# An adaLN transformer block on one core: the opening of the forward attention in written order on all engines, with the first two head pairs run together

## The chip, the cores and the metric

The kernel runs on one core of a Trainium2 chip. The time is that of one execution on the device, in microseconds; less is better. The profile is of one execution, taken by the hardware profiler, and its span runs from the first to the last instruction of that execution.

## What is computed

The reference is one block of a conditioned transformer, forward and backward (ten outputs: the block's result and nine gradients). B=1, S=2048, D=512, H=32 heads of 16, F=1792, all in bf16. Cut to the part that matters here:

```python
sa, ca, ga, sb, cb, gb = split(silu(c) @ w_mod)
h   = layernorm(x) * (1 + ca) + sa
q, k, v = split(h @ wqkv)                 # 32 heads of 16
o   = softmax(q @ k.T * 16**-0.5) @ v
x   = x + ga * (o @ wo)
x   = x + gb * mlp(layernorm(x) * (1 + cb) + sb)
# outputs: x and the gradients of A_x, wqkv, wo, w1, b1, w2, b2, c, w_mod
```

## The kernel before

The forward attention (`phase_fwd`, L265) works on four query chunks of 512 rows (`qc`), in each on eight groups of four heads (`g`), in each on two head pairs (`jp`). One such step is called `n` here: n=0 is chunk 0, group 0, first pair; n=1 the second pair; n=2 the first pair of group 1; n=16 opens the second query chunk. A step has 16 units, one per block of 128 keys (`kb`). A unit is two matmuls for the scores of two heads (L349, PSUM tile `st`), one exponential of 128x1024 on ACT (L352, to `pu`), and eight small matmuls of probabilities by values (PV, L314), two to four units later. At a step's end DVE divides by the row sums (L321, L322).

Into the units a `Background` of generators puts other matmuls: `step(1.2)` lets 1.2 matmuls' worth of credit into each unit of the first query chunk. For that chunk the generator is `gen_qkv` (L545). For each group g from 1 to 7 it makes the queries of chunk 0, the keys of all 2048 rows, then some small work, then queries of the group before for the other chunks. One projection of 512 rows is `gen_fm` (L519): four matmuls (L526), an eviction by DVE (L535), a store of the feature-major result to DRAM by SP (L536, `QTq_d` or `KTq_d`), and a token-major form: a DMA transpose on SP (L538, `ev_tm`, three buffers), a copy on POOL (L540) and a store from POOL's queue (L542). Each matmul is one `yield 1`. The small work is: the modulation for the later stages after group 2 (`gen_mod`); for groups 3 to 6 the transposed values of 512 rows (`gen_vt`, L575: four times two POOL copies into one of two `vpad` tiles, L583 and L584, and a DMA transpose on SP, L585, to `vT`; then one store on POOL's queue, L587); a scaled copy of weights on POOL for groups 3 to 6 (L565, `wm_s`), transposed on SP (L560) and stored by POOL's queue (L562, `WmT_d`) one group later. `gen_vt` lets a unit pass after each of its four blocks.

The queries of a step stand in two of four tiles `QTm`, zero outside one head's 32 rows. They are loaded for the step after by `load_q` (L295), two small DMAs on POOL's queue, which the program calls at unit 8 of each step. Only a step's first pair of a later chunk loads its keys from DRAM as well (`load_k`, L301); within the first chunk the keys are already in a tile.

The opening (`gen_open`, L389) comes before all this and runs into n=0. It loads x, the weights and part of `w_mod`, forms silu(c) and the first modulation columns (`silu_c`, `mod_cols`), runs two times ten matmuls that only warm PE, normalizes the first 512 rows (`norm`), transposes and scales them (`turn`, to `xm1T`), and projects keys and queries of group 0. Then come, chopped into n=0's units by the counts in `opening` (L330), for each further 512 rows: norm, transposes, a value matmul row by row (`values`, L472, four matmuls and an eviction into `Vaug`, by turns on ACT and DVE), and the key projection. `mps`, the PSUM pool of all these, has two buffers.

What sets the order: a `manual_schedule` for PE and SP around the forward and phase 5 (L160) keeps these two engines' instructions in the order of the program. DVE, ACT and POOL are ordered by the tile framework's scheduler, which may put an instruction, DMAs on POOL's queue among them, ahead of others written before it.

Of the kernel before, what the change touches and what calls it, by code (L numbers as in the profile page):

```python
# [10 lines left out]
F32 = mybir.dt.float32  # L11
# [10 lines left out]
EPS = 1e-5  # L22

# [81 lines left out]
class K:  # L105
# [159 lines left out]
    def phase_fwd(self):  # L265
# [21 lines left out]
        QTm = []  # L287
        for j in range(4):
            t = fw.tile([P, 512], BF16, name=f"QTm{j}")
            nc.vector.memset(t[:], 0.0)  # L290
            QTm.append(t)
# [36 lines left out]
        first = self.gen_open(Vaug, KT, QTm, stp)  # L328
        next(first)
        opening = [9 + DT + DT * 4] * (SC - 1) + [4 * DT + 1]  # L330
        for n, (qc, g, jp) in enumerate(order):
            if (qc, g, jp) == (1, 0, 0):
                bg.drain()
                self.close_qkv()
                self.open_mlp()
                bg.add(self.gen_weights())
            accb = accp.tile([P, 512], F32, name="accbank")
            acc = accb[:, 0:8 * (DH + 1)].rearrange("p (a s e) -> p a s e", a=2, s=4)
            self.cur_g = g
            for kb in range(ST):  # L340
                if kb == ST // 2 and n + 1 < len(order):
                    if n < 2 * NQ - 1 and jp == 1:
                        bg.until(g + 1)
                    load_q(*order[n + 1])
                    if jp == 1:
                        KTn = load_k(*order[n + 1][:2])
                stt = stp.tile([P, 2, 512], F32, name="st")
                for a in range(2):
                    nc.tensor.matmul(stt[:, a, :], lhsT=KT[:, kb * P:(kb + 1) * P], rhs=QTm[2 * jp + a][:],  # L349
                                     start=True, stop=True)  # L350
                pu = pup.tile([P, 2, 512], BF16, name="pu")
                nc.scalar.activation(pu[:], stt[:], ACT.Exp, scale=self.scale)  # L352
                u = (n, qc, g, jp, kb, acc, pu)
                now = n * ST + kb
                pend.extend((u, a, sub) for a in range(2) for sub in range(4))
                if n == 0:
                    left = opening[kb // 4]
                    take = -(-left // (4 - kb % 4))
                    opening[kb // 4] -= take
                    for _ in range(take):  # L360
                        next(first)
                rate = (1.14 if qc else 1.2) if n or kb > 11 else 0
                room = int((SPAN - 2 - bg.plan(rate)) / PVT)
                while pend:
                    age = now - (pend[0][0][0] * ST + pend[0][0][4])
                    if age < 2 or (room <= 0 and age < 4):
                        break
                    pv(pend.pop(0))
                    room -= 1
                if rate:  # L370
                    bg.step(rate)
            if jp == 1 and n + 1 < len(order):
                if n < 2 * NQ - 1:
                    bg.until(-(g + 1))
                KT = KTn
# [13 lines left out]
    def gen_open(self, Vaug, KT, QTm, stp):  # L389
# [28 lines left out]
        nc.sync.dma_start(self.wmod[:, :, 2 * D:6 * D], wmod_v[:, :, 2 * D:6 * D])  # L418
        self.silu_c(ps)
        warm = ps.tile([P, 512], F32, name="pps")  # L420
        for _ in range(10):
            nc.tensor.matmul(warm[:], lhsT=self.ones_b[:], rhs=QTm[0][:], start=True, stop=True)
        for t in (1, 0):
            nc.vector.memset(self.wpad0[t][:], 0.0)
        nc.vector.memset(Vaug[:, :, :, DH:DH + 1], 1.0)
        nc.scalar.memzero(wpads[1][:])
        self.mod_cols(ps, (0, 1))
        warm = ps.tile([P, 512], F32, name="pps")
        for _ in range(10):
            nc.tensor.matmul(warm[:], lhsT=self.ones_b[:], rhs=QTm[0][:], start=True, stop=True)  # L430
# [6 lines left out]
        def norm(s4):  # L437
            b = slice(s4, s4 + 4)
            for st in range(s4, s4 + 4):
                nc.vector.bn_stats(stats[:, st, :], x0[:, st, :])  # L440
                nc.vector.bn_aggr(mv[:, st, :], stats[:, st, :])
            nc.vector.tensor_scalar(ve[:, b], mv[:, b, 1], EPS, None, ALU.add)
            nc.gpsimd.tensor_tensor(self.rstd1[:, b], ve[:, b], self.mhalf[:], ALU.pow)
            if s4 == 0:
                nc.vector.scalar_tensor_tensor(nmr[:, b], mv[:, b, 0], -1.0, self.rstd1[:, b], ALU.mult, ALU.mult)
            for st in range(s4, s4 + 4):
                if s4 == 0 and st % 2 == 0:
                    nc.scalar.activation(xhat1[:, st, :], x0[:, st, :], ACT.Identity, bias=nmr[:, st:st + 1],
                                         scale=self.rstd1[:, st:st + 1])
                else:  # L450
                    nc.vector.tensor_scalar(xhat1[:, st, :], x0[:, st, :], mv[:, st, 0:1], self.rstd1[:, st:st + 1],
                                            ALU.subtract, ALU.mult)
            nc.sync.dma_start(self.xhat1_d.rearrange("(st p) d -> p st d", p=P)[:, b, :], xhat1[:, b, :])

        def turn(s4, k2):
            tp = ps.tile([P, 2, 512], BF16, name="pps")
            for kt in range(2):
                for k in range(4):
                    nc.tensor.transpose(tp[:, kt, k * P:(k + 1) * P],
                                        xhat1[:, s4 + k, (k2 + kt) * P:(k2 + kt + 1) * P], self.ident[:])  # L460
                yield 0
                yield 0
            for kt in range(k2, k2 + 2):
                dst = xm1T[:, kt, s4 * P:s4 * P + 512]
                if kt % 2:
                    nc.vector.tensor_scalar(dst, tp[:, kt - k2, :], self.opcaT[:, kt:kt + 1], self.mod_col(0)[:, kt:kt + 1],
                                            ALU.mult, ALU.add)
                else:
                    nc.scalar.activation(dst, tp[:, kt - k2, :], ACT.Identity, bias=self.mod_col(0)[:, kt:kt + 1],
                                         scale=self.opcaT[:, kt:kt + 1])  # L470

        def values(s4, s5):  # L472
            for st in range(s4, s5):
                pt = ps.tile([P, 512], F32, name="pps")
                for kt in range(DT):
                    nc.tensor.matmul(pt[:], lhsT=xm1T[:, kt, st * P:(st + 1) * P], rhs=wq[:, kt, 2 * D:3 * D],
                                     start=(kt == 0), stop=(kt == DT - 1))
                    if kt == DT - 1:
                        (nc.scalar.copy if st % 2 else nc.vector.tensor_copy)(Vaug[:, st, :, 0:DH], pt[:].rearrange("p (h d) -> p h d", d=DH))
                    yield 0  # L480

        norm(0)
        for t in (1, 0):
            nc.gpsimd.tensor_copy(self.wpad0[t][:].rearrange("p k (j e) -> p k j e", e=32)[:, :, :, 0:DH],
                                  wq[:, :, t * D:t * D + 4 * DH].rearrange("p k (j d) -> p k j d", d=DH))
        for k2 in range(0, DT, 2):
            for _ in turn(0, k2):
                pass
        for _ in self.gen_fm(ps, 1, 0, 0, dst=KT[:, 0:512]):
            pass  # L490
        for _ in self.gen_fm(ps, 0, 0, 0, masked=QTm):
            pass
        nc.scalar.memzero(wpads[0][:])
        for t in (1, 0):
# [4 lines left out]
        for t in self.vpads:  # L499
            nc.gpsimd.memset(t[:], 0.0)  # L500
            nc.gpsimd.memset(t[:, :, :, DH:DH + 2], 1.0)
        yield 0
        for s4 in range(4, ST, 4):
            norm(s4)
            for k in range(2):
                yield from turn(s4, 2 * k)
                yield from values(s4 - 4 + k, s4 - 3 + k)
            yield from self.gen_fm(ps, 1, 0, s4 * P, dst=KT[:, s4 * P:s4 * P + 512])
            yield 0
            yield from values(s4 - 2, s4)  # L510
        yield from values(ST - 4, ST)
# [7 lines left out]
    def gen_fm(self, ps, t, g, s0, dst=None, masked=None):  # L519
# [5 lines left out]
        for kt in range(DT):  # L525
            nc.tensor.matmul(pt[:], lhsT=self.wpads[t][:, kt, g, :] if g else self.wpad0[t][:, kt, :], rhs=self.xm1T[:, kt, s0:s0 + 512],  # L526
                             start=(kt == 0), stop=(kt == DT - 1))
            yield 1
        if masked:
            for j in range(2):  # L530
                nc.scalar.copy(masked[j][32 * j:32 * j + 32, :], pt[32 * j:32 * j + 32, :])
        if dst is None:
            ev = eb.tile([P, 512], BF16, name="ev_fm")
            dst = ev[:]
        nc.vector.tensor_copy(dst, pt[:])  # L535
        nc.sync.dma_start((self.QTq_d, self.KTq_d)[t][g, :, s0:s0 + 512], dst)  # L536
        tm = eb.tile([P, 4, 4, 32], BF16, name="ev_tm")
        nc.sync.dma_start_transpose(tm[:].rearrange("p s j e -> p s (j e)"), dst)  # L538
        tmc = eb.tile([P, 4, 4, DH], BF16, name="ev_tmc")
        nc.gpsimd.tensor_copy(tmc[:], tm[:, :, :, 0:DH])  # L540
        w = 4 * DH
        nc.gpsimd.dma_start((self.qtm_d, self.ktm_d)[t][g, :, s0 // P * w:(s0 // P + 4) * w],  # L542
                            tmc[:].rearrange("p s j d -> p (s j d)"))
# [1101 lines left out]
```

The softmax here doesn't subtract the row's maximum and nothing guards it: scores larger than these inputs give would overflow.

## Time and profile before

| | us |
|---|---|
| runs | 2647.73, 2642.17, 2647.95 (median 2647.73) |
| profiled execution: time, span | 2644.01, 2642.2 |
| PE busy | 2485.0 (94%) |
| ACT busy | 2297.5 (87%) |
| DVE busy | 1767.7 (67%) |
| POOL busy | 408.4 (15%) |

By stretches of the span (busy time of each engine; the PE clock is the granted one):

| stretch | PE | DVE | ACT | POOL | clock | DMA share |
|---|---|---|---|---|---|---|
| 0 to 33 us | 22.20 | 25.27 | 14.19 | 18.68 | 0.90 | 0.76 |
| 33 to 66 | 28.41 | 11.77 | 22.21 | 5.75 | 1.00 | 0.28 |
| 66 to 132 | 64.20 | 17.26 | 65.41 | 22.01 | 1.00 | 0.42 |
| 132 to 198 | 61.74 | 14.57 | 65.78 | 30.26 | 1.00 | 0.82 |
| 198 to 264 | 62.73 | 15.65 | 65.41 | 30.40 | 1.00 | 0.84 |

The first query chunk of the attention lasts until some 284 us, the forward's attention until 997 us. In a line of the timeline the columns are start, duration, engine, line of the program, operation, output and inputs, and in brackets the idle time of the engine before it and what ended it. Matmuls are pipelined, so durations of neighbours overlap; the distance of their starts is what one costs. A PE that is shown as busy need not be at its limit.

### The profile page before, as it was taken

The page shows a single profiled execution, that of the slowest core. Times are in us where ns is not written, and L with a number is a line of the kernel's source. Part 1 is how long each engine was busy: PE and PEld are TensorE (multiplying, and loading weights), DVE is VectorE, ACT ScalarE, POOL GpSimd, SP SyncE. Part 2 cuts the span into 40 slices and gives each one's busy share as a digit, 9 for nine tenths or more (in the row PEclk, how much of TensorE's full clock was granted, in tenths as well). Part 3 has the DMA queues.
Part 4 walks back from the last instruction along what each step waited for, and adds up shares of the span by engine and source line. Part 5 has one row for each costly group of instructions (what it writes and reads, how often), then busy time and mean ns, then how long its engine had stood idle before and what let it go on. Part 6 is the DMA issues. An engine that isn't in the chain of part 4 may idle for free. (4 is left out here: it accounts for less than half of the span.)

```text
span 2642.2 us, 76655 instructions
## 1 busy us (share of the span) xinstructions
PE 2485.0 (94%) x31000; PEld 1230.0 (47%) x31231; DVE 1767.7 (67%) x3653; ACT 2297.5 (87%) x3712; POOL 408.4 (15%) x678
## 2 busy tenths in 40 slices
PE   7999999999999999899999999999999999999997
PEld 3555555555555554663444344434444434443443
DVE  5222223423323344658999999999999999999867
ACT  5999999999999995318999999999999999999823
POOL 3344521310221121350000000000000000000031
PEclk9999999999999999999999999999999999999999
DMA  5488752440441245999999999999999999999986
GB/s 166 100 162 191 176 105 78 116 102 23 127 117 52 79 105 132 222 235 186 202 199 201 199 201 197 198 197 207 200 200 198 202 200 202 197 201 206 206 224 166
DMA packets 1197811, 441.16 MB, mean 167 GB/s; under 512 B 1134958, under 2 KB 1159024, under 8 KB 1197456
## 3 DMA queue, kind: packets, MB, share of 16 engines
q1 hardware_dynamic: 1167584, 347.42, 71.9%
q0 software_dynamic: 29872, 88.83, 11.5%
q8 instruction: 244, 4.00, 0.6%
q14 instruction: 111, 0.91, 0.1%
HBM read 83.30 MB, written 68.69 MB: 58 GB/s over the span
## 5 line engine op out<-in xcount | busy, mean ns | idle before, releaser
L1310 DVE TENSOR_TENSOR ds<-dp,pu 128x512 bf16<-128x512 f32 x2048 | 1243.7, 682 | 55.1 <-PE dp L1308 47.5
L1367 ACT ACTIVATE pu<-st 128x512 bf16<-128x512 f32 x2048 | 1082.4, 613 | 122.1 <-PE dp L1308 63.1
L352 ACT ACTIVATE pu<-st 128x1024 bf16<-128x1024 f32 x1024 | 944.6, 1072 | 18.4 <-PE st L349 15.8
L349 PE MATMUL st<-QTm,KTq 128*128 128x512 bf16 x1920 | 580.7, 378 | 30.0 <-ACT pu L352 7.2
L314 PEld LDWEIGHTS <-pu 128*128 128x128 bf16 x8192 | 347.5, 96 | 238.8 <-issue 4.0
L1287 PEld LDWEIGHTS <-dsT 128*128 128x128 bf16 x8192 | 245.1, 96 | 268.1 <-issue 205.6
L314 PE MATMUL accbank<-Vaug,pu 128*128 128x17 bf16 x8192 | 357.8, 171 | 7.0 <-ACT pu L352 0.3
L1308 PE MATMUL dp<-m,q 64*128 64x512 bf16 x1024 | 341.0, 386 | 0.9 <-DMA WmT<-WmT_d 0.9
L1308 PE MATMUL dp<-m,dOTq 64*128 64x512 bf16 x1024 | 338.5, 383 | 0.0
L1363 PE MATMUL st<-m,q 64*128 64x512 bf16 x1024 | 321.9, 385 | 7.9 <-ACT pu L1367 6.0
L1363 PE MATMUL st<-m,QTq 64*128 64x512 bf16 x1024 | 320.4, 383 | 6.4 <-ACT pu L1367 4.6
L349 PEld LDWEIGHTS <-KTq 128*128 128x128 bf16 x2048 | 193.7, 96 | 186.1 <-issue 133.5
L1418 POOL DMA_DIRECT2D O_tm<-O_d x2 | 1.8, 908 | 1316.3 <-PE accq L1287 1316.3
L1287 PE MATMUL accq<-q,dsT 128*128 128x16 bf16 x4096 | 150.7, 170 | 26.7 <-DMA dsT<-ds 26.3
L1287 PE MATMUL accq<-Kg,dsT 128*128 128x16 bf16 x4096 | 149.1, 170 | 27.8 <-DMA dsT<-ds 27.6
L1265 PE MATMUL acckv<-ds,q 128*16 128x512 bf16 x1024 | 155.4, 384 | 0.0
L1265 PE MATMUL acckv<-pu,q 128*16 128x512 bf16 x1024 | 155.4, 384 | 0.0
L1265 PE MATMUL acckv<-ds,Qg 128*16 128x512 bf16 x1024 | 155.1, 382 | 0.3 <-DVE ds L1310 0.2
L1265 PE MATMUL acckv<-pu,dOg 128*16 128x512 bf16 x1024 | 154.7, 382 | 0.0
L1328 ACT COPY dsT<-st 128x512 bf16<-128x512 bf16 x256 | 152.4, 595 | 1.1 <-PE st L1327 0.8
L321 DVE RECIPROCAL rl<-accbank 128x4 f32<-128x4 f32 x128 | 22.9, 179 | 150.5 <-PE accbank L314 150.4
L1363 PEld LDWEIGHTS <-q 64*128 64x128 bf16 x1024 | 58.2, 94 | 123.9 <-issue 104.5
(322 smaller groups left out, 2634.4 us busy)
## 6 DMA issues: line engine op xcount, KB each, us to landing
KTq<-KTq_d POOLq DMA_DIRECT2D x24, 512.0 KB, 3.8
duT_d<-auT POOLq DMA_DIRECT2D x4, 1792.0 KB, 8.8
aT_d<-rT POOLq DMA_DIRECT2D x4, 1792.0 KB, 12.9
KTq_d<-KTq SPq DMA_DIRECT2D x32, 128.0 KB, 2.0
QTq_d<-ev_fm SPq DMA_DIRECT2D x32, 128.0 KB, 3.1
VTq_d<-vT POOLq DMA_DIRECT2D x4, 1024.0 KB, 6.3
O_d<-O POOLq DMA_DIRECT2D x4, 1024.0 KB, 6.2
m<-KTq_d SPq DMA_DIRECT2D x32, 128.0 KB, 3.5
```

The costliest lines, as they stand in the source:

```text
L314: nc.tensor.matmul(acc[:, a, sub, :], lhsT=pu[:, a, sub * P:(sub + 1) * P], rhs=Vaug[:, kb, h, :], start=(kb == 0 and a == 0 and sub == 0) ...
L321: nc.vector.reciprocal(self.rl[:, st0:st0 + 4, h], acc[:, a, :, DH])
L349: nc.tensor.matmul(stt[:, a, :], lhsT=KT[:, kb * P:(kb + 1) * P], rhs=QTm[2 * jp + a][:], start=True, stop=True)
L352: nc.scalar.activation(pu[:], stt[:], ACT.Exp, scale=self.scale)
L1265: nc.tensor.matmul(acckv[r:r + DH, :], lhsT=T[n][:, ib, col:col + DH], rhs=src[:, a, :], start=(ib == 0), stop=(ib == ST - 1))
L1287: nc.tensor.matmul(accq[:, ib, a, :], lhsT=dsT[:, (i * 2 + a) * 4 + sub, :], rhs=T["K"][:, 4 * c + sub, col:col + DH], start=(c == 0 and i ...
L1308: nc.tensor.matmul(dp[:], lhsT=T["dOT"][rd, ib * P:(ib + 1) * P], rhs=masked["VT"][2 * jp + a][rd, 512 * c:512 * (c + 1)], start=True, sto ...
L1310: nc.vector.tensor_tensor(dsg[:, i, a], dp[:], pu[:, a, :], ALU.mult)
L1328: nc.scalar.copy(dsT[:, 0:4, :], tp[:])
L1363: nc.tensor.matmul(stt[:], lhsT=T["QT"][rs, q], rhs=masked["KT"][2 * jp + a][rs, c0:c0 + 512], start=True, stop=True)
L1367: nc.scalar.activation(pu[:, a, :], stt[:], ACT.Exp, scale=self.scale)
L1418: nc.gpsimd.dma_start(O_tm[:, b, :], tm_v(self.O_d)[:, b, :])
```

## The change

All of DVE, ACT and POOL join PE and SP in written order, from the opening to the end of the first query chunk. n=0 and n=1 are run as one block of 32 units: for each 512 keys first four units of n=0, then four of n=1. The work between the units is fixed by hand, eight slots per 512 rows: four value rows, two halves of the transposes, the key projection, and one slot for four background matmuls (`bg.take`). n=0 gets its queries in two extra tiles `QTo`, so that `QTm` is free for n=2. The token-major half of every projection in the opening is put on a list (`late`), and is issued in n=2, one per unit. Memsets, weight padding and the silu chain come first; the weight padding of group 0 goes from POOL to ACT; ten and ten warm-up matmuls become fourteen; the scaling of transposes is split differently between ACT and DVE; three value rows in four are evicted by DVE. In `gen_fm` the eviction now comes with the fourth matmul and not at the step after it.

```diff
+        self.late = []
+        self.cur_g = 0
+        es = ExitStack()
+        es.enter_context(tc.manual_schedule(engines=ALL))
+        QTo = []
+        first = self.gen_open(Vaug, KT, QTm, QTo, bg)
         next(first)
-        opening = [9 + DT + DT * 4] * (SC - 1) + [4 * DT + 1]
-        for n, (qc, g, jp) in enumerate(order):
+        units = [(n, 4 * s + k) for s in range(SC) for n in range(2) for k in range(4)]
+        for i, (n, kb) in enumerate(units):
+            if i == len(units) // 2:
+                bg.until(1)
+                load_q(*order[2])
...
+                nc.tensor.matmul(stt[:, a, :], lhsT=KT[:, kb * P:(kb + 1) * P], rhs=(QTm[2 + a] if n else QTo[a])[:],
+                                 start=True, stop=True)
...
+            nc.scalar.activation(pu[:], stt[:], ACT.Exp, scale=self.scale)
+            u = (n, 0, 0, n, kb, accs[n], pu)
+            next(first)
+            pend.extend((u, a, sub) for a in range(2) for sub in range(4))
+            while len(pend) > 16:
+                pv(pend.pop(0))
+        next(first)
+        late, self.late = self.late, None
+        bg.until(-1)
+        KT = self.KT_next
+        for n, (qc, g, jp) in list(enumerate(order))[2:]:
             if (qc, g, jp) == (1, 0, 0):
                 bg.drain()
+                es.close()
...
+                if late:
+                    late.pop(0)()
+                rate = 1.14 if qc else 1.2
...
+        for s4 in range(0, ST, 4):
+            n4 = s4 + 4
+            last = n4 == ST
+            value(s4)
             yield 0
...
+            for h in range(2):
+                if not last:
+                    tp = ps.tile([P, 2, 512], BF16, name="pps")
+                    turn(n4, 2 * h, tp)
+                    scale(n4, 2 * h, tp, (2 * h,))
+                else:
+                    bg.take(DT)
...
+                yield 0
+            if not last:
+                fm(1, 0, n4 * P, dst=KT[:, n4 * P:n4 * P + 512])
...
+            yield 0
+            if not last:
+                bg.take(DT)
+            yield 0
...
         nc.sync.dma_start((self.QTq_d, self.KTq_d)[t][g, :, s0:s0 + 512], dst)
...
+        def token_major():
+            tm = eb.tile([P, 4, 4, 32], BF16, name="ev_tm")
+            nc.sync.dma_start_transpose(tm[:].rearrange("p s j e -> p s (j e)"), dst)
+            tmc = eb.tile([P, 4, 4, DH], BF16, name="ev_tmc")
+            nc.gpsimd.tensor_copy(tmc[:], tm[:, :, :, 0:DH])
...
+        if self.late is None:
+            token_major()
+        else:
+            self.late.append(token_major)
+        yield 1
```

## The prediction

> **What bounds the kernel now.** I read the page's costliest groups, then the timeline of ACT, then PE's and POOL's timelines, then the landing times of the transfers. The group that counts is the softmax exponential, 1024 instructions:
>
> ```profile
> L352 ACT ACTIVATE pu<-st 128x1024 bf16<-128x1024 f32 x1024 | 944.6, 1072 | 18.4 <-PE st L349 15.8
> ```
>
> The columns are busy time, mean ns, and idle time before it. From 66 to 264 us the stretches show ACT busy 65.4 to 65.8 us in each 66: there it is the bound, with one exponential every 0.92 us (62.77 us for 68) and 14.7 us for a head pair's 16. Almost all the 18.4 us of idle lies in the opening:
>
> ```profile
> 25.38 1.02 ACT L352 ACTIVATE pu<-st 128x1024 bf16<-128x1024 f32 x1 [0.67 <-PE st L349]
> 26.30 0.77 ACT L469 ACTIVATE xm1T<-pps,modT,opcaT 128x512 bf16<-128x512 bf16 x1
> ...
> 62.06 1.02 ACT L352 ACTIVATE pu<-st 128x1024 bf16<-128x1024 f32 x1 [1.66 <-PE st L349]
> 62.98 0.58 ACT L479 CAST Vaug<-pps 128x512 bf16<-128x512 f32 x1
> 63.45 12.26 ACT L352 ACTIVATE pu<-st 128x1024 bf16<-128x1024 f32 x13
> ```
>
> Columns are start and duration. The first pair's 16 exponentials take 25.4 to 63.4 us, the second pair's run back to back, and the third pair (n=2) starts at 78.4 us (the 33rd exponential). So a gain can only come before 78.4; after it ACT has nothing to give. PE's prices, warm, are the distances between starts here:
>
> ```profile
> 44.77 0.61 PE L459 MATMUL pps<-ident,xhat 128*128 128x128 bf16 x8
> 45.21 1.03 PE L476 MATMUL pps<-wqkv,xm1T 128*128 128x512 bf16 x4
> ...
> 52.92 0.35 PE L314 MATMUL accbank<-Vaug,pu 128*128 128x17 bf16 x8
> 53.12 0.59 PE L349 MATMUL st<-QTm,KTq 128*128 128x512 bf16 x2
> 53.55 1.24 PE L476 MATMUL pps<-wqkv,xm1T 128*128 128x512 bf16 x5
> ```
>
> Eight transposes take 0.44, a unit's eight PV 0.20, its two score matmuls 0.43 (0.215 each), so a V tile or a projection (four) 0.86.
>
> The other thing to read is POOL around 166 us, n=8, with SP beside it:
>
> ```profile
> 166.48 1.00 POOL L295 DMA_DIRECT2D QTm<-QTq_d  x2 [0.54 <-PE st L349]
> 168.47 0.40 POOL L540 COPY ev_tmc<-ev_tm 128x256 bf16<-128x256 bf16 x1 [0.99 <-DMA ev_tm<-KTq]
> 169.17 0.57 POOL L542 DMA_DIRECT2D ktm_d<-ev_tmc  x1 [0.29 <-POOL ev_tmc L540]
> 173.11 1.01 POOL L562 DMA_DIRECT2D WmT_d<-wm_t  x1 [3.37 <-DMA wm_t<-wm_s]
> ...
> 178.93 0.40 POOL L583 COPY vpad<-Vaug 128x256 bf16<-128x256 bf16 x1 [1.88 <-DMA vT<-vpad]
> ```
>
> ```profile
> 164.86 0.33 SPq L536 DMA_DIRECT2D KTq_d<-KTq  x1
> 165.28 1.19 SPq L538 DMA_TRANSPOSE ev_tm<-KTq  x1
> 166.52 1.51 SPq L560 DMA_TRANSPOSE wm_t<-wm_s  x1
> 168.08 10.06 SPq L585 DMA_TRANSPOSE vT<-vpad  x4
> ```
>
> POOL stands still at each copy until a transpose has landed. The loads of the next pair's queries (L295) were put in front: the load issued at 166.48 is written at unit 8 of n=8 (about 174), but POOL's order was free, so it went out as soon as its buffer was. SP's order is already the written one, and nothing overtakes its 10 us of vT.
>
> **What the Trainium skill says.** "PSUM — Partial Sum Buffer", section Engine vs sequencer instructions: the queues of ScalarE, VectorE and GpSimdE are strictly first in, first out. The trace agrees: POOL's copy at 178.93 waited 1.88 us for a transpose and nothing ran in between. "TensorE: Matmul & The Clock Gate", Part 1: an idle window of some 3.4 us halves PE's clock. Here:
>
> ```profile
> 332.00:333.00 1.00, 0.07 (x1) 0.10 (x2) 0.00 (x0) 0.46 (x1) 1.00 (x2) 0.72 0.77 171
> 333.00:334.00 1.00, 1.00 (x3) 0.33 (x3) 0.00 (x0) 0.00 (x0) 0.95 (x2) 0.50 1.24 288
> ```
>
> These are stretches of 1 us with PE first after the length and PEclk third from the end: after 1.65 us of PE idle the clock is 0.50, and ACT, idle for 2.43, then loses another 0.44.
>
> **The change, part by part: opening.** Start: the silu chain now stands first on DVE (scT_b at about 4 us instead of 11.7), then six memsets (0.27 each) to 5.3. Four bn_stats (1.28 a pair) with aggregates reach 9.0, the norms 10.6. PE's 14 warm-up matmuls at the cold pitch 0.43 end at 10.0, mod_cols (0.99) at 11.0, 16 transposes (1.83) at 12.8. Two ACT scales (0.77, 0.66) reach 14.1, Q's four matmuls cold 16.3, DVE's ev_fm (0.69) and the new 32-row copy 17.3, the scores 18.0. The copy has no row; between 0.1 and 0.7 (the 128-row cast), I take 0.3. First exponential **18.0 against 25.4: -7.4** (16.5 if PE warms early, 20 if not).
>
> Loop: PE's 32 units cost 32 x 0.63 = 20.2, V 16 x 0.86 = 13.8, transposes 6 x 0.44 = 2.6, K 3 x 0.86 = 2.6, the five bg.take (exactly the 20 matmuls of group 1) 4.3: 43.5. ACT (32 x 0.92 + 6 x 0.7 + 4 x 0.6 = 36) lies beside it. Each of three K projections waits some 0.8 for the second scale, behind exp 0.92, scale 0.66, exp 0.92 on ACT (2.4). The last two units are bound by ACT (0.6). Cold clock at first: nothing to 5, I take 2. Sum 48.5 against 53.0 (78.4 - 25.4): **-4.5**. DVE's work per 512 tokens (four norms 0.4, four bn_stats 0.64, four casts 0.69, two scales 0.54, small ones 0.9: 8.9) lies beside 11.6 of PE. Together n=2 starts at 66.5: **-11.9**. The deferred half of gen_fm costs the opening nothing; it is paid next.
>
> **After the opening: POOL in written order until the second query chunk.** DVE and ACT lose nothing there: DVE is busy 14 to 17 us in each 66, its written order is PE's, ACT has only exponentials. On POOL, load_q is written at unit 8 and now waits behind all written before it. A pair's queries must be in 14.1 us after the previous pair's start (14.7 less 0.6 for the scores). A projection ending in unit k reaches SP 1.8 us after that unit's start (n=7 starts at 152.1, its unit 12 at 163.1, SP at 164.86), its transpose is issued at 2.2, lands 3.2 later (median of ev_tm; 2.4 to 6.4), POOL's copy and store take 1.24, and load_q lands 2.6 later (0.5, then 2.1 median): 9.2 after the unit's start. Ending in unit 5 it is in time, 6 gives a wait of 0.6, 7 one of 1.5. Counting the yields of gen_qkv at 1.2 per unit (a projection is 4; a V block holds every second unit) from an empty credit at n=2 gives what stands ahead of each load_q:
> - n=2: eight deferred transposes and two projections. SP can start them 1.3 us ahead; at 1.2 each with ev_tm's three buffers the tenth goes out at 11.8 and lands at 15.3, store 16.6, loads land at 19.2: wait **5.1**.
> - n=6: wm_s (1.6), four vpad copy pairs of group 3 (0.7; the third and fourth wait for vT of the first and second, 3.9 median), VTq_d's store behind the fourth's landing (16.3), one projection (18.8). Loads land at 21.4: **7.3**.
> - n=8, 10, 12: wm_t lands at 7.0, WmT_d 8.0, wm_s 9.6, copies 11.0, then vT again: 14.2 and 15.7, copies 16.4. Loads land at 19.0: **4.9 each, 14.7**.
> - n=9, 11, 13 end a projection in unit 7 (4.5 in all); n=3, 5, 14 in unit 6 (1.8).
> - n=15: keys of the next chunk behind load_q, 512 KB in 4.9: 1.2.
>
> Sum 34.6, and 0.44 of cold clock for each of five long waits: 36.8. Bounds: with every landing at its minimum some 20; with backlogged ones (4 us and more) and a whole cold window each, 48. None can be a gain, since ACT had under 1 us of idle between 78 and 284.
>
> **Sum:** 36.8 - 11.9 = +24.9 on the span of 2642.2. That execution took 2644.0; the others shown are 2647.7, 2642.2 and 2647.9. On the median: 2672.6.
>
> **The rivals.**
> - **B, the opening's gain stays.** For it: SP and POOL are half idle, and in this trace load_q for n=10 and n=12 left POOL 9.3 and 9.9 us into the pair before (190.92 and 220.97) without a wait. If waits come to 2 us: 2647.7 - 11.9 + 2 = 2638. It decides if load_q gets out within 11.5 us of each pair's start. Against it: four places where the written queue alone is longer than that.
> - **C, they cancel.** Landings near their minima and phases that fall well: waits of 12, 2648.
> - **D, the opening is no better:** PE has 43.5 us of work in it; if DVE or ACT in written order hold PE up by 1.5 us per 512 tokens (6), the loop gains nothing and the result is 2679. I count it within the slower case.
>
> **Numbers.** Slower as worked out 0.55 (own range 2655 to 2692), B 0.26, C 0.19. A measurement of this kernel tells about 0.3% (7.9 us) from no change, so: faster 0.26, same 0.19, slower 0.55. The range 2636 to 2690 leaves out a third of B and the top of the slower case.
>
> **What would show it.** First exponential near 18 and the 33rd near 66.5 confirm the opening. ACT idle of 5 us ahead of the first exponential of n=3, n=7, n=9, n=11 and n=13, released by score matmuls that themselves waited for L295, confirms the rest; L295 late behind the vpad copies is the sign on POOL. I am wrong if ACT is busy through those borders, or if load_q still overtakes on POOL.

## The result and the profile after

The changed kernel takes 2681.14 us (median; 2680.0 to 2683.12) against 2647.84 us for the kernel before (2642.17 to 2656.08), a ratio of 1.0124 with a 95% interval of 1.0097 to 1.0152. It is slower by 33.3 us; the profiled spans, 2679.2 and 2642.2, differ by 37.0.

The opening did get shorter, and the steps after it longer. On the page, the groups of later exponentials and of later score matmuls (busy time, mean ns, idle time before them):

```profile
L378 ACT ACTIVATE pu<-st 128x1024 bf16<-128x1024 f32 x992 | 914.2, 1076 | 50.9 <-PE st L375 50.0
L375 PE MATMUL st<-QTm,KTq 128*128 128x512 bf16 x1859 | 570.8, 382 | 61.9 <-DMA QTm<-QTq_d 31.0
```

The exponential itself costs what it did (1076 ns against 1072). New is the idle time before it: 50.9 us where all 1024 exponentials had 18.4, most of that in the opening. ACT waits for scores, and these for the query load. Where it happens stands in ACT's timeline:

```profile
20.43 1.02 ACT L346 ACTIVATE pu<-st 128x1024 bf16<-128x1024 f32 x1 [1.51 <-PE st L343]
...
69.81 14.78 ACT L378 ACTIVATE pu<-st 128x1024 bf16<-128x1024 f32 x16
90.72 1.02 ACT L378 ACTIVATE pu<-st 128x1024 bf16<-128x1024 f32 x1 [6.13 <-PE st L375]
...
161.22 1.02 ACT L378 ACTIVATE pu<-st 128x1024 bf16<-128x1024 f32 x1 [10.11 <-PE st L375]
...
198.84 1.02 ACT L378 ACTIVATE pu<-st 128x1024 bf16<-128x1024 f32 x1 [6.64 <-PE st L375]
...
234.46 1.02 ACT L378 ACTIVATE pu<-st 128x1024 bf16<-128x1024 f32 x1 [3.15 <-PE st L375]
...
270.84 1.02 ACT L378 ACTIVATE pu<-st 128x1024 bf16<-128x1024 f32 x1 [3.59 <-PE st L375]
...
322.98 1.94 ACT L378 ACTIVATE pu<-st 128x1024 bf16<-128x1024 f32 x2 [3.75 <-PE st L375]
```

The first line is the first exponential (25.38 before), the second the start of n=2 (78.4 before), so the opening gives 8.6 us. The others are the starts of n=3, 7, 9, 11, 13 and 16: each is a border between two head pairs. With the smaller ones at n=10 (1.49), n=12 (0.90) and n=14 (2.88) the border waits sum to 38.6 us. Between 78 and 284 us the kernel before had under 1 us of them.

PE's view of the waits from 66 to 330 us (total, times, longest) names what ends them:

```profile
PE st L375 <- DMA QTm<-QTq_d: 31.0, 9, 9.7
PE st L375 <- ACT pu L378: 4.7, 15, 0.4
PE st L375 <- DMA KTq<-KTq_d: 3.6, 1, 3.6
```

And why the load is late stands in POOL's timeline around the longest wait, n=7, with SP's beside it:

```profile
140.09 1.55 POOL L644 TENSOR_SCALAR wm_s<-wqkv,opcaT 128x1536 bf16<-128x1536 bf16 x1
...
145.71 0.40 POOL L662 COPY vpad<-Vaug 128x256 bf16<-128x256 bf16 x1 [2.69 <-DMA vT<-vpad]
...
148.66 0.40 POOL L662 COPY vpad<-Vaug 128x256 bf16<-128x256 bf16 x1 [2.21 <-DMA vT<-vpad]
...
153.02 0.97 POOL L666 DMA_DIRECT2D VTq_d<-vT  x1 [3.62 <-DMA vT<-vpad]
...
155.24 1.02 POOL L292 DMA_DIRECT2D QTm<-QTq_d  x2
```

```profile
142.36 8.30 SPq L664 DMA_TRANSPOSE vT<-vpad  x4
```

SP's own waits from 139 to 157 us (total, times, longest):

```profile
SPq L664 <- POOL vpad L663: 9.8, 3, 6.9
```

POOL is busy for a few tenths at a time and idle for 2 to 4 us in between: it stands behind a transpose on SP that itself stands behind POOL's copies. The query load (L292) leaves at 155.24, after all of that. n=7 could have started at about 151; its first exponential is at 161.22.

Last, the opening's first instructions on DVE and on POOL:

```profile
2.20 1.60 DVE L185 CAST ident_f<-ident 128x128 f32<-128x128 bf16 x1 [1.04 <-POOL ident masks.py:199]
2.44 1.35 DVE L210 CAST cT<-pps 128x4 f32<-128x4 bf16 x1
```

```profile
2.21 0.94 POOL L441 MEMSET vpad<- 128x1024 bf16 x1
3.10 0.52 POOL L963 MEMSET dgb_acc<- 128x512 f32 x1
3.57 0.14 POOL L442 MEMSET vpad<- 128x64 bf16 x1
```

In the kernel before, these two casts took 0.22 and 0.15 us. Here both end at 3.80, when POOL's memsets are through (3.71).

### The profile page after: what moved, and what is told of

It reads as the page before. It is cut to its first block, busy times and chain, and to the rows that moved or that the text cites. A ratio compares the mean times of both kernels' runs of the same rounds, so it can differ in the third digit from the quotient of the medians.

```text
span 2679.2 us, 76647 instructions
## 1 busy us (share of the span) xinstructions
PE 2489.9 (93%) x30995; PEld 1229.0 (46%) x31225; DVE 1774.2 (66%) x3662; ACT 2296.4 (86%) x3710; POOL 407.2 (15%) x675
## 5 line engine op out<-in xcount | busy, mean ns | idle before, releaser
L378 ACT ACTIVATE pu<-st 128x1024 bf16<-128x1024 f32 x992 | 914.2, 1076 | 50.9 <-PE st L375 50.0
L375 PE MATMUL st<-QTm,KTq 128*128 128x512 bf16 x1859 | 570.8, 382 | 61.9 <-DMA QTm<-QTq_d 31.0
```

## The experiments

The theory was that POOL's written order holds back the query loads. The rivals were that written order on DVE or ACT costs the time, that the long opening block does, or that a wait taken away comes back elsewhere. Ratios are to the kernel before on the same chip.

**1. POOL out of the written order.** The change with only one engine taken from its list.

```diff
-ALL = {..., mybir.EngineType.Activation, mybir.EngineType.Pool}
+ALL = {..., mybir.EngineType.Activation}
```

> The changed kernel, but POOL is left to the scheduler throughout; PE, SP, DVE and ACT stay in written order. Theory A (the loads of the next queries stand behind other work in POOL's written order; nothing else is lost): the 44 us of ACT idle between 66 and 330 us fall to under 5, the third head pair still starts near 70 us, and the time is 2636 to 2644, some 8 under the kernel before (the gain of the opening). Rival R1 (the written order of DVE and ACT, or the deferred transposes, make the waits): at least 20 us of idle remain and the time stays above 2660.

Measured: 2647.2 us, ratio 1.0003 (0.9991 to 1.0016). ACT's idle (the brackets from the start of n=2 to 330 us, summed) fell from 45.1 us to 5.5 (3.31 of it at n=14), with DVE and ACT still in written order through the whole first chunk. But n=2 started at 75.35, 5.5 us later than in the change. POOL's timeline of this kernel:

```profile
9.71 4.07 POOL L503 COPY wpad<-wqkv 128x448 bf16<-128x448 bf16 x8 [4.09 <-DMA wqkv<-in_A_wqkv_dram]
13.74 1.41 POOL L465 TENSOR_TENSOR rstd<-ve,mhalf 128x2 f32<-128x2 f32 x2
```

Left free, POOL took 4 us of weight copies ahead of the small `rstd` (one over the standard deviation) that the first normalization waits for. In the changed kernel the two `rstd` ran at 8.15 and 9.76. By these traces the opening wants POOL in order and the steps after it want POOL free. The waits went nearly as the theory said; the time expected, 2636 to 2644, was missed by 3 us, for the opening lost 5.5, which the theory had not thought of.

**2. Written order for the opening alone.** DVE, ACT and POOL are released before n=2.

```diff
         KT = self.KT_next
+        es.close()
         for n, (qc, g, jp) in list(enumerate(order))[2:]:
...
                 bg.drain()
-                es.close()
```

> The changed kernel, but the written order of DVE, ACT and POOL ends with the opening's 32 units, before the third head pair. Theory A: the opening alone is worth the 8 to 9 us by which the third head pair starts earlier (69.8 against 78.4), so 2637 to 2644, with less than 5 us of ACT idle from 66 to 330. Rival R2 (what the opening gains is given back to the deferred transposes in n=2, which now crowd SP and the DMA engines): an idle of 4 us or more at the start of n=3, time 2643 to 2650.

Measured: 2638.64 us, ratio 0.9972 (0.9962 to 0.9982), n=2 at 71.49, and 4.8 us of waits, the longest 2.94 at n=14, as theory A had it. There is none at n=3, so the deferred transposes cost nothing once POOL is free, and rival R2 fell. With the same edits in the opening this is some 40 us less than the change (1.52 points of the ratio). At n=14 PE waits for the query load again; why it leaves late there was not traced. The three kernels that leave POOL free after the opening (experiments 1, 2 and 12) wait 2.9 to 3.5 us there, and the kernel before 0.2.

**3. POOL's written order without the change.** The kernel before, with POOL in written order from n=2 to the end of the first chunk.

```diff
+            if n == 2:
+                es.enter_context(tc.manual_schedule(engines={PE, SP, Pool}))
...
                 bg.drain()
+                es.close()
```

> The kernel before with its own opening; only POOL is put in written order from the third head pair to the second query chunk. Theory A: the loss alone, without the deferred transposes: waits of 4 to 10 us at n=9, n=11 and n=13, 1 to 3 at some others, none at n=3, together 20 to 35 us, so 2666 to 2683. Rival R1 (the waits need DVE and ACT in written order or the new opening): within 5 us of the kernel before.

Measured: 2677.81 us, ratio 1.0128 (1.0111 to 1.0145). ACT's timeline of it has the same borders (n=7, 9, 11, 13):

```profile
157.08 1.02 ACT L356 ACTIVATE pu<-st 128x1024 bf16<-128x1024 f32 x1 [6.94 <-PE st L353]
...
198.70 1.02 ACT L356 ACTIVATE pu<-st 128x1024 bf16<-128x1024 f32 x1 [10.23 <-PE st L353]
...
235.24 1.02 ACT L356 ACTIVATE pu<-st 128x1024 bf16<-128x1024 f32 x1 [4.80 <-PE st L353]
...
271.32 1.02 ACT L356 ACTIVATE pu<-st 128x1024 bf16<-128x1024 f32 x1 [4.41 <-PE st L353]
```

There is none at n=3, where the change has its deferred transposes; n=15 and n=16 have 1.5 and 3.4. PE's waits from 76 to 330 us are for the same loads:

```profile
PE st L353 <- DMA QTm<-QTq_d: 27.4, 10, 9.9
```

Together with the second experiment this shows the cause: POOL in order after the opening costs some 31 us by itself, with nothing of the change's opening in the kernel. The price of the waits is rather higher, for in this trace n=2 started at 74.8, 3.6 us sooner than in that of the kernel before, though the program of the opening is the same; the scheduler may have ordered it otherwise.

**4. The load called earlier, POOL still in order.** In the first chunk `load_q` is called at unit 0 of a step whose next queries are long projected, at unit 4 otherwise. There `bg.until`, which has the background finish that projection first, comes four units earlier with it.

```diff
-                if kb == ST // 2 and n + 1 < len(order):
+                if kb == (ST // 2 if qc else 4 * jp * (g < NQ - 1)) and n + 1 < len(order):
```

> The changed kernel with all engines in written order, but load_q is called at unit 0 of a step where the next step has the same keys, and at unit 4 where it has new ones (unit 0 before the second query chunk), up to the second query chunk. Theory A: position in the queue is all that matters, so the waits at the first units of n=3, 7, 9, 11 and 13 (6.1, 10.1, 6.6, 3.2, 3.6 us in the changed kernel) go to under 0.5 each, and the time is 2637 to 2646. Rival R1 (POOL's or SP's throughput, or the DMA engines, are the limit, so that earlier issue only moves the wait): more than 20 us of ACT idle remain between 66 and 330 us, time above 2660.

Measured: 2655.94 us, ratio 1.0044 (1.0028 to 1.006). The waits at n=3, 7, 9, 11 and 13 are gone. Others are there now, at n=8 (2.08), 10 (5.84), 12 (3.02) and 14 (4.26):

```profile
199.56 2.12 ACT L378 ACTIVATE pu<-st 128x1024 bf16<-128x1024 f32 x2 [5.84 <-PE st L375]
```

```profile
193.44 0.40 POOL L613 COPY ev_tmc<-ev_tm 128x256 bf16<-128x256 bf16 x1 [4.39 <-DMA ev_tm<-ev_fm]
...
195.90 1.03 POOL L292 DMA_DIRECT2D QTm<-QTq_d  x2
```

These steps begin a new group, whose queries are projected only in the step before. An early call stands behind copies again, which wait for SP's transposes. Theory A was right about the five borders that it names and 10 us too low in the time. Of the rival's two signs one came, barely (20.1 us of ACT idle from 66 to 330), and one did not (a time under 2660); its claim, that the wait moves, holds at the other borders.

**5. Only n=3's load moved.** The same condition with `ST // 2 if n > 2 else 0`: the load for n=3 goes ahead of the deferred transposes.

> The changed kernel with one load moved: in n=2 alone load_q is called at unit 0, ahead of the deferred transposes, all else in written order at its place. Theory A: the 6.9 us at the start of n=3 (6.1, 0.5 and 0.3) go, the other waits stay within 1 us each, and the time is 2672 to 2676. Rival R3 (the wait only moves, as it did in part when all loads went earlier: the backlog that the wait let run down now meets n=3's own load): 3 us or more appear at the start of n=4 and the time stays above 2677.

Measured: 2684.81 us, ratio 1.0146 (1.0126 to 1.0166). The 6.1 us at n=3 are gone, and 4.70 us have come at n=4 and 3.35 at n=15, while n=14 fell from 2.88 to 0.2. The wait moved, as the rival said.

**6. No query load at all in the first chunk.** DVE copies the 32 rows of each head from the projection's own tile; POOL stays in order. In a group's first step, and in n=15, the call stands at unit 0.

```diff
+            if qc == 0:
+                for j in (2 * jp, 2 * jp + 1):
+                    nc.vector.tensor_copy(QTm[j][32 * j:32 * j + 32, :], self.q_ev[32 * j:32 * j + 32, :])
+                return
             for j in (2 * jp, 2 * jp + 1):
                 nc.gpsimd.dma_start(QTm[j]...
...
-                if kb == ST // 2 and n + 1 < len(order):
+                if kb == (0 if qc == 0 and (jp == 0 or g == NQ - 1) else ST // 2) and n + 1 < len(order):
...
+        if t == 0 and s0 == 0:
+            self.q_ev = ev
```

> The changed kernel with all engines in written order, but in the first query chunk the queries of the next step are copied by DVE (two copies of 32x512) from the projection's own bf16 tile, at unit 0 or 8; no load from DRAM, so nothing stands on POOL or SP. The loads and keys of the second query chunk are called at unit 0 of n=15. Theory A (only the place of these loads in the queues of POOL and SP makes the waits; DVE and ACT in written order cost nothing): ACT idle from 70 us to the end of n=15 under 2 us, n=2 at 69 to 71, time 2635 to 2641. Rival R1 (written order on DVE, or the density of transposes on the DMA engines, also holds up PE): 8 us or more of idle remain, time above 2645.

Measured: 2650.97 us, ratio 1.0015 (1.0004 to 1.0026). Every wait for `QTm` from n=3 to n=16 is gone. In its place, in the middle of n=11 and n=13, stand 5.18 and 4.38 us. (4.12 more stand in n=17, past the stretch in written order; PE waits there for another DMA, `fT`.) PE's waits, then DVE and SP in n=11:

```profile
PE pps L598 <- DVE ev_fm L609: 8.7, 3, 4.3
```

```profile
215.47 0.69 DVE L609 CAST ev_fm<-pps 128x512 bf16<-128x512 f32 x1 [7.39 <-DMA ev_tm<-ev_fm]
```

```profile
203.31 8.96 SPq L670 DMA_TRANSPOSE vT<-vpad  x4
212.37 0.53 SPq L613 DMA_DIRECT2D QTq_d<-ev_fm  x1
```

DVE may not evict the next projection: one of the three `ev_fm` buffers is still held for a transpose that stands on SP behind the four of vT, and these stand behind POOL's copies. PE then waits for DVE. So the query load was one exit of a chain, and closing it led the delay to the next. Rival R1's signs came (over 8 us of idle, a time above 2645); the buffers it had not named.

**7. The memsets moved.** The sixth kernel, with the `vpad` memsets placed after the first statistics instead of first on POOL.

> The kernel of the run before with one more edit: POOL's memsets of the two vpad tiles stand after the first statistics instead of first in the opening. Theory V (a POOL memset beside DVE's first two casts stretches these from 0.22 and 0.15 to 1.60 and 1.35 us, and this is the part of the 2.4 us by which the first exponential came later than forecast that is not the clock): the two casts take under 0.4 each, the first warm-up matmul starts near 3.9 instead of 5.2, and the first exponential comes 0.8 to 1.5 us earlier than in the run before; the whole time falls by about as much, too little to be told by itself. Rival (the casts are slow for another reason, as the wait on the identity or a cold start): they stay above 1 us.

Measured: 2649.99 us, ratio 1.0011 (0.9999 to 1.0023). The casts take 0.23 and 0.16 us:

```profile
1.77 0.23 DVE L185 CAST ident_f<-ident 128x128 f32<-128x128 bf16 x1 [0.62 <-POOL ident masks.py:199]
2.36 0.16 DVE L210 CAST cT<-pps 128x4 f32<-128x4 bf16 x1 [0.36 <-PE pps L208]
```

The first exponential is at 19.55 instead of 21.07, n=2 at 68.93 instead of 70.27. That the memsets stretch the casts is shown. But the two traces also differ in PE's clock, which is 0.50 until some 23 us in the sixth kernel's and until some 17 in this one, so not all of the 1.5 us comes from the memsets. Over all traces with this opening in written order, six with the memsets first have the first exponential at 20.35 to 21.07, and five with them moved at 19.34 to 20.29: the means differ by 0.95 us. The 1.0 us of whole time is within the intervals.

**8 and 9. The next links of the chain.** The seventh kernel with six `ev_fm` buffers (`bufs=6`), and, apart from that, with WmT's transpose and store and `wm_s` after the four vpad steps in place of ahead of them.

> The previous variant (queries of the first chunk copied by VectorE, vpad memsets after the first statistics) with six buffers for ev_fm instead of three. Theory C (one chain: POOL's written order holds the vT transposes on SP, these hold the projections' transposes behind them, these hold the ev_fm buffers, and so VectorE and PE): with six buffers the two waits of ScalarE in n=11 and n=13 (5.5 and 4.1 us) are gone or under 1 us each, and the time falls by 7 to 10 us against the previous variant, to 2639 to 2643. Rival M (the wait moves on once more, to the next thing behind SP, such as the query copies by POOL or the output's stores): a new wait of 3 us or more in n=7 to 16, the time stays within 4 us of the previous variant, 2646 to 2651.

> The same previous variant (three ev_fm buffers), but each group's transpose and store of WmT and its wm_s come after the four vpad steps instead of ahead of them in the written order. Theory C1 (the vpad copies stood behind WmT's store and wm_s on POOL, and that started the chain): the ev_fm waits in n=11 and n=13 shrink from 5.5 and 4.1 to under 2 us each; time 2640 to 2644. Rival C2 (the four vpad steps with two buffers are slow on their own, each transpose 2 to 3 us after its copy, and hold SP without any help of WmT): the waits stay at 4 us or more each, time 2648 to 2652.

Six buffers: 2643.75 us, ratio 1.0004 (0.9993 to 1.0015). The waits in n=11 and n=13 are gone, and 7.31 us have come at n=16, for the keys, which POOL loads as well:

```profile
PE st L379 <- DMA KTq<-KTq_d: 7.2, 1, 7.2
```

The wait moved on, as rival M said, though the time is in neither range, and the ratio fell by 0.0007 only. The later WmT: 2642.97 us, ratio 0.9988 (0.9975 to 1.0001). The wait in n=13 is gone, that in n=11 is 6.12. The four vT transposes hold SP for 7.65 us there with no WmT ahead of them, so each of C1 and C2 is half right about the waits, and C1 about the time.

**10. The same WmT move in the change itself.**

> The kernel after, with only the WmT block moved behind the four vpad steps. Theory C1 (WmT's store and wm_s on POOL are a good part of what the query loads stand behind): the waits of ScalarE at the starts of n=7, 9, 11 and 13 (10.1, 6.6, 3.2, 3.6 us) fall by 2 to 5 us each, in all by 8 to 14; time 2667 to 2674. Rival C2 (the loads stand behind vT's four steps and its store, whatever is ahead of these): those waits stay within 1 us of what they were; time 2679 to 2683.

Measured: 2676.28 us, ratio 1.0128 (1.0101 to 1.0155), not told from the change's 1.0124. The waits at n=7, 9, 11 and 13 fell as C1 wanted in all, to 8.71, 2.07, 0 and 0, by 12.7 us. At n=10, 12 and 14 they rose to 4.49, 4.06 and 3.19, from 5.3 in all to 11.7, and 1.55 came at n=15. All border waits together are 34.4 us where the change has 38.6. Most of what one border lost came back at another, and C1's time, 2667 to 2674, was missed.

**11. All four remedies together,** POOL in order throughout.

> All engines in written order through the whole first query chunk, with four edits together: queries of the first chunk copied by VectorE, vpad memsets after the first statistics, six ev_fm buffers, WmT's block behind the four vpad steps. Theory S (the written order has a remedy for each of its waits: six buffers take the 6.1 us wait of n=11, the later WmT block takes the 7.3 us wait for the keys at n=14): no wait of ScalarE over 1.5 us from n=3 to n=15; time 5 to 10 us under the kernel before, ratio 0.996 to 0.998. Rival M (SP's transposes and POOL's copies are one line of work that comes late whatever is reordered, so a wait of 5 us or more comes back at another border): ratio 0.9985 to 1.0005.

(The wait for the keys that this text puts at n=14 stands at n=16.) Measured: 2643.65 us, ratio 0.9995 (0.9982 to 1.0009). No wait over 1 us is left from n=3 to n=15, as theory S said, but 6.25 us stand at n=16. (The next one, 2.37 at 332 us, the kernel before has too, 2.43.) POOL ahead of n=16:

```profile
271.43 0.40 POOL L619 COPY ev_tmc<-ev_tm 128x256 bf16<-128x256 bf16 x1 [2.59 <-DMA ev_tm<-ev_fm]
...
275.79 1.04 POOL L296 DMA_DIRECT2D QTm<-QTq_d  x2
276.83 0.58 POOL L302 DMA_DIRECT2D KTq<-KTq_d  x1
```

The keys of the next chunk have lain in DRAM for 200 us, and their load goes out at 276.83, in its written place. In the kernel before it went out at 258.2, since the scheduler had put it ahead. The wait came back at another border, as rival M said, and the ratio lies in its range. With four remedies, POOL in order is not better than the kernel before.

**12. The opening alone in order, and the memsets moved:** the second and the seventh experiment's edits together.

> Written order of VectorE, ScalarE and POOL only up to n=2, and the vpad memsets after the first statistics. Theory V (the memsets stretch VectorE's first two casts by 1.3 us each, of which 1.3 us lies on the path to the first exponential): first exponential 1.3 us earlier than with the written opening alone, n=2 at 70.1 instead of 71.5, time 2636 to 2638.5, 8 to 11 us under the kernel before. Rival (the end of the opening is set by PE's work and not by its start): n=2 at 71.2 to 71.8 and the time unchanged at 2638 to 2640.

Measured: 2633.98 us beside 2644.45 for the kernel before, ratio 0.9961 (0.9948 to 0.9974): some 10 us faster than before and 1.6% faster than the change. n=2 starts at 69.68, and two waits are left, at n=14 and at 329 us, where the kernel before waited 2.43:

```profile
69.68 6.53 ACT L378 ACTIVATE pu<-st 128x1024 bf16<-128x1024 f32 x7
...
251.12 1.02 ACT L378 ACTIVATE pu<-st 128x1024 bf16<-128x1024 f32 x1 [3.50 <-PE st L375]
...
329.52 15.69 ACT L378 ACTIVATE pu<-st 128x1024 bf16<-128x1024 f32 x17 [1.62 <-PE st L375]
```

Against the second experiment n=2 came 1.8 us earlier, where theory V had 1.4, though the first exponential only 0.7 (20.29 against 20.97) and not 1.3. Here too the clock differs: 0.50 from 12 to 18.8 us in this trace, from 16 to 25 in that of the second experiment, so a part of the 1.8 us may be the clock's. That the memsets gain time here is likely but not shown, for the two ratios' intervals overlap.

## Why the prediction was right

Direction, mechanism and range held: the opening gains, POOL's written order costs more, and the time of 2681.1 lies in the likeliest case. The range, 2636 to 2690, is wide and takes in rival C and most of rival B as well; what speaks for the prediction is where the waits stand. All five waits came at the borders named (at n=11 and n=13 with 3 us, not 5), released by score matmuls that waited for the query loads. The cause was tested from both sides (experiments 2 and 3). Rival B's figure, 2638, is near what the kernel took once POOL was free after the opening (2638.64, of another set of runs; some 8 us under the kernel before where B has 10), so B failed on its condition, a load out within 11.5 us of each step's start. D, the opening no better, is refuted by the change itself, with n=2 8.6 us earlier. C's time, waits that cancel the gain, is what the kernels with several remedies came to (experiments 6 to 9 and 11), by edits that C did not have in view.

What of the opening's 8.6 us comes from running two pairs together and what from the written order was not separated, but for POOL's part (experiment 1).

By its terms, in us:

| step | forecast | measured |
|---|---|---|
| first exponential | 18.0 | 20.43 |
| opening loop, to n=2 | 48.5 | 49.4 |
| gain at n=2 | 11.9 | 8.6 |
| n=3 | 5.1 | 6.1 |
| n=7 | 7.3 | 10.1 |
| n=9, 11, 13 | 14.7 | 6.6 + 3.2 + 3.6 = 13.4 |
| n=10, 12, 14 | 4.5 | 1.5 + 0.9 + 2.9 = 5.3 |
| n=4, 6, 15 | 1.8 | none |
| n=16 | 1.2 | 3.75 |
| clock after the waits | 2.2 | 6.2 |
| sum of waits and clock | 36.8 | 44.8 |
| net, on the span | +24.9 | +37.0 |

The sum of the waits less the gain is 36.2; the other 0.8 us of the span was not traced. Three terms were too small.

- **The start.** The silu chain was to be done at about 4 us on DVE; it was done at 4.88, since the two casts ahead of it took 1.60 and 1.35 us. The 16 transposes end at 13.7 where I had 12.8, and over all traces the memsets are worth about this much (experiment 7). The four scales that follow were priced as two on ACT beside DVE, 1.3 us; in the trace they run one after the other, ACT, DVE, ACT, and end at 16.2, 2.4 us after the transposes:

```profile
13.55 0.78 ACT L484 ACTIVATE xm1T<-pps,modT,opcaT 128x512 bf16<-128x512 bf16 x1 [2.66 <-PE pps L477]
14.36 1.00 DVE L487 TENSOR_SCALAR xm1T<-pps,opcaT,modT 128x512 bf16<-128x512 bf16 x2 [1.32 <-ACT xm1T L484]
15.39 0.78 ACT L484 ACTIVATE xm1T<-pps,modT,opcaT 128x512 bf16<-128x512 bf16 x1 [1.07 <-DVE xm1T L487]
```

  Why each waits for the other was not tested. Another 0.4 lies between the end of the query projection (18.3) and the first exponential, 2.1 where I had 1.7: a 0.57 us cast to `QTo` on ACT stands ahead of DVE's `ev_fm`.
- **The longest waits.** The place in the queue was right, the landing was not. The load left POOL 17.0, 19.0 and 17.0 us after the start of the step ahead of n=3, n=7 and n=9, where I had 16.6, 18.8 and 16.4. But I took 2.1 us for its landing, the median of the trace of before over the whole forward (1.8 to 12.4); at these borders it was 2.7, 4.7 and 3.2. At n=7 (150 to 162 us) the 1 MB store of vT, 6.0 us to land, and transposes, 4.8, were in flight with it; that these slowed it is likely, but no run tested it. At n=11 and n=13 the load left after 13.5 and 13.8 us, not 16.4, and landed in 2.8 and 3.0: so the close sum for n=9, 11 and 13, 13.4 against 14.7, is in part luck, two errors that cancel. For n=16 I priced only the keys' transfer, at 4.9 us; the load left POOL 2.7 us late, behind a copy, and took 6.3.
- **The clock.** I took 0.44 us for each of five waits, from one place in the trace of before. The bracketed idle that follows the waits sums to 1.3 at n=7, 1.9 at n=11 and 6.2 in all. The granted clock is still 0.50 for a while after PE's first matmul: until 93.1 us at n=3 (PE starts at 89.4), until 164.7 at n=7 (160.1), until 239.8 at n=11 (232.6), so for 3.6 to 7.2 us. In that time most units are short of scores by some 0.5 us, not one unit alone. "TensorE: Matmul & The Clock Gate" in the Trainium skill, Part 1, has the clock fall after an idle window of some 3.4 us; in this trace it fell some 2 us into PE's idle at n=3 and some 4 us at n=7, and in the one that the prediction shows before 1.65 us were over. These are two stretches of 1 us at n=7, with PE first and the clock third from the end:

```profile
154.00:155.00 1.00, 0.00 (x0) 0.00 (x0) 0.00 (x0) 0.00 (x0) 0.70 (x2) 0.74 0.40 72
164.00:165.00 1.00, 1.00 (x13) 0.49 (x11) 0.34 (x1) 0.44 (x1) 0.00 (x0) 0.64 0.00 0
```

Three small waits didn't come, at n=4, 6 and 15. At n=6 and n=15 the load left POOL 10.9 and 10.8 us after the step before began, where the forecast comes to 12.1, and was in time. At n=4 the load left after 12.7, but that step itself, slowed by the cold clock, took 16.1 us instead of 14.7. Nor are the borders independent: in experiments 5 and 10 waits rose at one border when they fell at another. A sum of separate borders, as in the forecast, is an estimate and no more. The time itself is 8.5 us over the forecast; the span by 12.1, since the profiled execution of before (2644.0) was among the quicker ones.

## What to carry to other kernels

A written order on an engine that issues DMAs orders its queue as well: a load written late waits for everything before it, and copies that wait for transposes on another queue make that long. Before fixing an order, list for each load what is written ahead of it and when its buffer is free; where the scheduler had hoisted it, leave that engine free and fix the order only where it pays, here the opening. When a wait that is taken away comes back at the next border, stop mending single waits: look for the chain that feeds them all, here POOL's copies and SP's transposes that wait for each other.

## What was not expected of the hardware

Memsets on POOL stretched a cast on DVE from 0.23 us to 1.60, until POOL was through (experiment 7). "SBUF — State Buffer" in the Trainium skill, section SBUF: two separate sides, says that the two engines share a pair of ports as an exclusive lock, and that one blocks fully while the other holds it; of DVE's instructions it names those in a two-port mode. The cast ending at 3.80, within 0.1 us of the last memset (3.71), agrees. No run here shows whether the cast ran in such a mode, nor which of the four memsets beside it held it. The second cast, 1.35 us, ends with the first and may only have stood behind it on DVE.
